# A gated FNet and GEGLU layer in split fp32: sum tiles in two places of their own, weight sums in place, loads and splits at fixed points of a pair

## The chip, the cores and the metric

The kernel runs on one core of a Trainium2 chip. The metric is device time in microseconds, the median over separate runs. One further run is recorded by the hardware profiler; all rows shown here come from that one execution. TensorE (PE) multiplies, VectorE (DVE) and ScalarE (ACT) prepare operands and take results, GpSimd (POOL) issues the stores and SyncE (SP) issues the loads.

## The reference

```python
g = sigmoid((x * gate_w).sum(-1, keepdims=True))     # x: 2048 x 640
a = Re(DFT_seq(DFT_hidden(x)))                       # dense real and imaginary DFT matrices
b = (gelu(x @ w_gate) * (x @ w_up)) @ w_down         # 640 -> 1728 -> 640, tanh gelu
return g * a + (1 - g) * b
```

Everything is fp32. The matrices of both DFTs are inputs.

## The kernel before, in words

**Arithmetic.** An fp32 product is made of three matmuls on fp32r operands: each operand is split into a high part (`high`, a copy on ScalarE, L75) and a low part (`low`, a subtraction on VectorE, L78), and `mm3` (L84 to L88) multiplies high by high, high by low and low by high into one PSUM bank of 128 x 512. Around that stand Strassen and Winograd forms: two blocks of 128 hidden units and two halves of a sequence half are combined so that fewer block products are needed, and sums of weights and of inputs are multiplied instead of the blocks themselves. Names with S, s or T, t are such sums.

**Stages.** The first stage splits x and its sums and computes the left-over blocks. Then come the gate and up products in pairs of hidden blocks. `gate_up` makes f = 1 and 2 one by one; `pair_first` and `chain` make pair p = 1; `whole_pair` (L508) makes each of the pairs p = 2, 3, 4, 5, which hold the blocks f = 2p+1 and 2p+2. After the pairs come the down products (the k stage), the DFT over the sequence (the c stage) and the DFT over the hidden dimension (the u stage).

**A whole pair.** `whole_pair` is a generator: it writes the pair's matmuls, seeds, copies and sums in a fixed order and yields numbers u = 3, 7, 10 ... 68. Between the yields the loop at L1151 to L1205 writes the other work of the pair: loads (`load_raw` for the weight tiles wa and wb of the next pair, `load_cross` for the input sums xx), `chain_parts` (the weight sums ws and their split, and wd), `fifth_parts` (the sums fs over the ws of both blocks, and their split fh), `pair_parts` (vs, vh, vl, ve, vq) and `plain_parts` (wp) for the next pair, and `extras`: the sums of a down weight chunk (`sum_wd`: loaded as dr and da, stored as wsd) and the logits of the gate (`load_z`: xz). Within the pairs the order on TensorE is as written (`in_order(PE)`); the order on the other engines is made by the scheduler of the framework, from the order in which the work is written and from what each instruction waits for.

A bank is copied with `seed` (L441): ScalarE copies a PSUM bank into another bank, and both go on as sums of their own. The seed px10 (L568) stands between the product s3 by t3 and the product a22 by t4: the latter accumulates on the copy.

**Places.** SBUF is handed out in slots of 4 KB per partition (`slot`, tag s4, 48 of them), 12 tiles of 2 KB (`mtile`) and 6 small ones (`wsmall`). A slot's next tile waits until the last reader of its former one is through, a store too. The s5 tile of a block (L539) holds the sum from which both its gated results are made; its four stores to DRAM (hT, by `keep`, L331) come at the pair's end, from L690 to L705. A down weight's sums are made into a further slot (`sums_left`, L707) and stored from there.

Of the kernel before, what the change touches and what calls it, by code (L numbers as in the profile page):

```python
# [30 lines left out]
def kernel(  # L31
# [33 lines left out]
    def slot(dt, shape, name):  # L65
        return pool.tile(shape, dt, tag="s4", name=name, bufs=48)

# [74 lines left out]
    def load_x(tp):  # L142


        n = f"{tp}"
        B, r = {}, {}
        src = xt[2 * tp : 2 * tp + 2]

        def tiles(t):
            for k in (1, 2):  # L150
                r[k, t] = pair(F32, f"xr{n}{k}{t}")
                B[k, t] = hl(f"x{n}{k}{t}")
            if t == 1:
                r[5], B[5] = pair(F32, f"xr{n}5"), hl(f"x{n}5")

        def load(t):
            for k in (1, 2):
                nc.sync.dma_start(r[k, t], src[t - 1, 2 * k - 2 : 2 * k].rearrange("d p c -> p d c"))
            nc.sync.dma_start(r[5][:, t - 1], src[t - 1, 4])

        def piece(d, t):

            raw = r[1 + d // 2, t][:, d % 2] if d < 4 else r[5][:, t - 1]
            return raw, src[t - 1, d], xpart(B, d, t)

        def tsum(i):
# [3 lines left out]
            tt(r[f"T{i}"], r[a], r[b], op=ALU.subtract)  # L170
# [12 lines left out]
        return B, tiles, load, piece, tsum, his, lows  # L183
# [52 lines left out]
    def chain_parts(f, raw, W):  # L236

        ra, rb = raw
        sm, *c = wchunk(f"ws{f}")
        g01, g23, u23 = ra[:, 0:2], ra[:, 2:4], ra[:, 5:7]  # L240
# [7 lines left out]

        def parts():
            split(*c, sm)  # L250
            split(d[:, 0], d[:, 1], rb[:, 1])
# [15 lines left out]
    def pair_parts(p, r0, r1):  # L267

        a, b = (r[:, 0:4].rearrange("q (j k) c -> q k j c", j=2) for r in (r0, r1))
        sm = slot(F32, [P, 4, 2, P], f"vs{p}")  # L270
        h, l = slot(F32R, [P, 4, 2, P], f"vh{p}"), slot(F32R, [P, 4, 2, P], f"vl{p}")
        e, q = slot(F32R, [P, 2, 4, P], f"ve{p}"), pool.tile([P, 2, 2, P], F32R, tag="m", name=f"vq{p}", bufs=12)
        tt(sm[:, 0], b[:, 0], b[:, 1], op=ALU.add)
        tt(sm[:, 2], a[:, 0], b[:, 0], op=ALU.subtract)
        tt(sm[:, 1], sm[:, 0], a[:, 0], op=ALU.subtract)
# [10 lines left out]
    def fifth_parts(p, W0, W1):  # L286
# [37 lines left out]

    tcross = {}

    def load_cross(J, i):
# [180 lines left out]
    def whole_pair(p, WP, Ws, raws):  # L508
# [98 lines left out]
        Z[0, 1] = seed(za, f"pz01{p}")  # L607
        yield 29
        fifth(Z[0, 0], 0, "u5", 1, 0)
        nc.scalar.activation(s5[0][:, 0], Z[0, 0], AF.Copy)  # L610
        plus(s5[0][:, 0], X[0, 0])
        prod(X[1, 0], 1, "S2", "T2", 0)
        state(1, 0)
# [11 lines left out]
        nc.scalar.activation(s5[0][:, 1], Z[0, 1], AF.Copy)  # L625
        plus(s5[0][:, 1], X[0, 1])
        m(Z[1, 0], 3, "a22", "t4")
# [128 lines left out]
    def gate_tile(row, tp, name):  # L756

        g = pair(F32, name)
        nc.sync.dma_start(g.rearrange("p t c -> p (t c)"), row[:, 2 * tp * T : 2 * (tp + 1) * T].to_broadcast([P, 2 * T]))
        return g  # L760

    def load_z(sb):

        r = slot(F32, [P, D], f"xz{sb}")
        nc.sync.dma_start(r, xz[sb])
        return lambda: nc.vector.tensor_tensor_reduce(r, r, gwb, 1.0, 0.0, ALU.mult, ALU.add, z[:, sb : sb + 1])

# [3 lines left out]
    def load_xn(sp):  # L771
# [9 lines left out]
        nc.sync.dma_start(r2, xn[sp, :, 3:5])  # L781
        sm = slot(F32, [P, 4, 256], f"xs{sp}")
        a11, a12, a22, a21 = r1[:, 0], r1[:, 1], r2[:, 0], r2[:, 1]
# [24 lines left out]
    def split_c(i):  # L808
# [3 lines left out]
        if b:  # L812
            s1 = pair(F32, f"csa{i}")
            tt(s1[:, 0], r1[:, 1], r1[:, 0], op=ALU.subtract)  # L814
            tt(s1[:, 1], r2[:, 0], r1[:, 1], op=ALU.subtract)  # L815
            s2 = pair(F32, f"csb{i}")
            tt(s2[:, 0], r2[:, 0], s1[:, 0], op=ALU.subtract)
# [16 lines left out]
    def load_k(i):  # L834
# [13 lines left out]
        elif b:  # L848
            nc.sync.dma_start(r[:, 0:2], wd[k, :, 6:8])
            nc.sync.dma_start(r[:, 2:8], wsd[k][:, 0:6])  # L850
            src = hT[tp][k]
        else:
            nc.sync.dma_start(r[:, 0:6], wd[k, :, 0:6])
            nc.sync.dma_start(r[:, 6:8], wsd[k][:, 6:8])
            src = hA[tp][k]
# [6 lines left out]
    def split_k(i):  # L862
# [18 lines left out]
        else:  # L881
            h, l = slot(F32R, [P, 8, P], f"kh{n}"), slot(F32R, [P, 8, P], f"kl{n}")
            split(h, l, r)
            names = ("A22", "S1", "S2", "S3") if b else ("A11", "A12", "e5", "S4")
            W = {name: (at((h, l), 2 * q), at((h, l), 2 * q + 1)) for q, name in enumerate(names)}
# [194 lines left out]
    sq = [lambda k=k: sum_wd(k) for k in range(NK)]  # L1080

    def extras(sums, logits):
        todo = [sq.pop(0)() for _ in range(sums) if sq]
# [6 lines left out]
    for f in (1, 2):  # L1090
        s5 = pair(F32, f"s5{f}")
        work = [gate_up(f, W, Bs[tp], tp, s5[:, tp]) for tp in range(2)]
# [28 lines left out]
    for i in range(2):  # L1121
        s5 = pair(F32, f"s5{f + i}")
        work = [chain(f + i, Ws[i], Bs[tp], tp, s5[:, tp], X[i, tp], s1[i, tp]) for tp in range(2)]
        for step in range(4):
# [13 lines left out]
            if (i, step) == (0, 2):  # L1138
                nraws = load_raw(f + 2), load_raw(f + 3)
            if (i, step) == (1, 0):  # L1140
                raws = nraws
                WP = pair_parts(2, raws[0][0], raws[1][0])
            if (i, step) == (1, 1):
                Ws = [plain_parts(f + 2 + i, raws[i][0]) for i in range(2)]
                for J in (2, 1):
                    load_cross(J, 1)
            if (i, step) == (1, 2):
                load_cross(2, 2)
            if (i, step) == (1, 3):
                load_cross(1, 2)  # L1150
    for p in range(2, NK):  # L1151
        f = 2 * p + 1
        more = p < NK - 1
        for J in (2, 1):
            load_cross(J, 4)
        with in_order(PE):
            for u in whole_pair(p, WP, Ws, raws):
                if u == 3:
                    parts = [chain_parts(f + i, raws[i], Ws[i]) for i in range(2)]
                if u == 7:  # L1160
                    parts[0]()
                    parts.append(fifth_parts(p, *Ws))
                    load_cross(3, 1)
                if u == 10:
                    WP[3] = parts[2]()
                    load_cross(3, 2)
                if u == 16:
                    parts[1]()
                    load_cross(3, 4)
                if u == 19:  # L1170
                    todo = extras(1, 2)
                if u == 23 and more:
                    nraws = load_raw(f + 2), load_raw(f + 3)
                if u == 29:
                    for do in todo[:1]:
                        do()
                    todo = todo[1:] + extras(p > 2, 2)
                if u == 38:
                    for do in todo:
                        do()  # L1180
                if more:
                    if u == 47:
                        nWP = pair_parts(p + 1, nraws[0][0], nraws[1][0])
                    if u == 56:
                        nWs = [plain_parts(f + 2, nraws[0][0])]
                        for J in (2, 1):
                            load_cross(J, 1)
                    if u == 62:
                        nWs.append(plain_parts(f + 3, nraws[1][0]))
                        load_cross(2, 2)  # L1190
                    if u == 65:
                        load_cross(1, 2)
                else:
# [377 lines left out]
```

## Time and profile before

| | |
|---|---|
| Median of three runs | 1031.0 us (1028.17, 1031.0, 1031.08) |
| The profiled execution | 1027.66 us |
| Its span | 1025.8 us |
| Mean granted clock of TensorE | 0.998 |
| TensorE busy | 1016.0 us, 99% of the span |
| VectorE busy | 807.0 us, 79% |
| ScalarE busy | 489.3 us, 48% |
| GpSimd busy | 140.7 us, 14% |
| DMA traffic | 265 MB, mean 258 GB/s |

The span is what the profiler saw between the first and last instruction; the execution's own time is 1.9 us longer. Busy shares hide where a stage waits. The 20-us windows of the trace show 89 or 90 matmuls in each full window but four: the first one (73), 200 to 220 us (78), 240 to 260 us (72), and 1000 to 1020 us (110, where the last ones are narrower).

In the rows of the timeline, the columns are start in us, duration in us, engine, source line, operation, written tile, read tiles, and shapes; a bracket gives the idle time before the instruction and what ended it. In the waits, the columns after the colon are total us, times and the longest wait. In the windows they are the stretch, its length, and busy us and instruction count of PE, PEld (weight loads), DVE, ACT and POOL, then the granted clock, the DMA share and GB/s. In the list of DMA issues the last number is the median time from issue to landing. In grouped rows of one tile they are the minimum, median and maximum duration in ns.

### The profile page before, as it was taken

How to read it: one execution, taken by the hardware profiler on the slowest of the kernel's cores; microseconds unless marked ns; L12 is line 12 of the kernel's file. 1: busy time of each engine (PE TensorE's matmuls, PEld its weight loads, DVE VectorE, ACT ScalarE, POOL GpSimd, SP SyncE). 2: the span in 40 equal slices, each digit the busy share in tenths (PEclk: the TensorE clock that was granted, in tenths of full speed). 3: DMA queues.
4: the chain of work that ended last, by engine and by line, in shares of the span. 5: the costliest groups of instructions: out<-in, count | busy, mean ns of one | idle time of the engine just before them, and what ended most of it. 6: DMA issues, size and time to landing. Idle time of an engine off the chain costs nothing.

```text
span 1025.8 us, 13092 instructions
## 1 busy us (share of the span) xinstructions
PE 1016.0 (99%) x4488; PEld 838.5 (82%) x4488; DVE 807.0 (79%) x1134; ACT 489.3 (48%) x654; POOL 140.7 (14%) x251
## 2 busy tenths in 40 slices
PE   9999999999999999999999999999999999999998
PEld 7888888787888888888888888888888888888887
DVE  6998797778785958976898976796598769697784
ACT  5445365454455547566355343443444345365430
POOL 0123131212121200100010011102100200021013
PEclk9999999999999999999999999999999999999999
DMA  8368697878698988867856679667966777897748
GB/s 300 120 211 290 248 326 269 298 258 308 235 336 310 301 285 278 282 257 254 322 190 237 212 244 331 228 216 259 324 231 215 269 270 286 292 323 217 276 92 134
DMA packets 87666, 265.00 MB, mean 258 GB/s; under 512 B 11088, under 2 KB 19312, under 8 KB 87600
## 3 DMA queue, kind: packets, MB, share of 16 engines
q1 hardware_dynamic: 65392, 194.47, 55.6%
q0 software_dynamic: 22064, 69.50, 19.8%
q8 instruction: 35, 0.57, 0.2%
q14 instruction: 31, 0.25, 0.1%
q10 hardware_dynamic: 144, 0.20, 0.1%
HBM read 194.38 MB, written 69.75 MB: 257 GB/s over the span
## 4 chain that ended last, share of the span: by engine, by line
PE 81%; issue 13%; POOL 4%; DMA 1%; DVE 1%; ACT 0%; POOLq 0%; DVEq 0%; ACTq 0%
PE pX L86 3%; PE pX L87 3%; PE pX L88 3%; PE pL L87 3%; PE pL L88 3%; PE pL L86 3%; PE pZ L88 2%; PE pZ L87 2%; PE pZ L86 2%; PE pV L87 2%; PE pV L88 2%; PE pV L86 2%; POOL hA L332 2%; POOL hT L332 1%; PE pR L87 1%
## 5 line engine op out<-in xcount | busy, mean ns | idle before, releaser
L75 ACT ACTIVATE ch<-csa 128x1024 fp32r<-128x1024 f32 x32 | 34.0, 1063 | 85.7 <-DVE csa L815 69.2
L75 ACT ACTIVATE ch<-cra 128x1024 fp32r<-128x1024 f32 x32 | 33.9, 1058 | 47.7 <-DVE cl L78 22.4
L78 DVE TENSOR_TENSOR cl<-crb,ch 128x1024 fp32r<-128x1024 f32 x32 | 39.1, 1221 | 16.3 <-ACT ch L75 14.7
L78 DVE TENSOR_TENSOR cl<-cra,ch 128x1024 fp32r<-128x1024 f32 x32 | 39.1, 1223 | 15.5 <-ACT ch L75 10.2
L88 PE MATMUL pL<-ch,xal 128*128 128x512 f32 x128 | 49.8, 389 | 0.0
L87 PE MATMUL pL<-cl,xah 128*128 128x512 f32 x128 | 49.8, 389 | 0.0
L86 PE MATMUL pL<-ch,xah 128*128 128x512 f32 x128 | 49.3, 389 | 0.0
L75 ACT ACTIVATE ch<-crb 128x1024 fp32r<-128x1024 f32 x32 | 33.8, 1057 | 25.0 <-PE pL L87 8.6
L78 DVE TENSOR_TENSOR cl<-csb,ch 128x1024 fp32r<-128x1024 f32 x32 | 39.2, 1224 | 3.1 <-ACT ch L75 1.2
L332 POOL DMA_DIRECT2D hA<-s x48 | 26.1, 544 | 104.7 <-DVE s L685 71.8
L78 DVE TENSOR_TENSOR cl<-csa,ch 128x1024 fp32r<-128x1024 f32 x32 | 39.0, 1220 | 1.2 <-ACT ch L75 0.8
L75 ACT ACTIVATE ch<-csb 128x1024 fp32r<-128x1024 f32 x32 | 34.0, 1063 | 9.3 <-DVE csb L818 5.8
L78 DVE TENSOR_TENSOR kl<-kw,kh 128x1024 fp32r<-128x1024 f32 (+1 forms) x26 | 31.4, 1209 | 5.8 <-ACT kh L75 5.8
L684 ACT ACTIVATE s<-s 128x512 f32<-128x512 f32 x20 | 12.7, 633 | 48.5 <-DVE s L530 33.0
L75 ACT ACTIVATE kh<-kw 128x1024 fp32r<-128x1024 f32 (+1 forms) x26 | 27.1, 1042 | 11.1 <-DVE kw L873 7.1
L928 POOL DMA_DIRECT2D out<-ks x12 | 6.5, 540 | 166.7 <-DVE ks L927 166.1
L332 POOL DMA_DIRECT2D hT<-s x48 | 26.0, 541 | 20.1 <-DVE s L703 5.5
L814 DVE TENSOR_TENSOR csa<-cra 128x512 f32<-128x512 f32 x32 | 21.9, 685 | 8.2 <-DMA wsu<-u2s 4.7
L86 PEld LDWEIGHTS pL<-ch,xah 128*128 128x128 f32 x128 | 24.0, 188 | 5.0
L87 PEld LDWEIGHTS pL<-cl,xah 128*128 128x128 f32 x128 | 24.0, 188 | 5.0
L88 PEld LDWEIGHTS pL<-ch,xal 128*128 128x128 f32 x128 | 24.0, 188 | 5.0
L1273 POOL DMA_DIRECT2D uA<-c x8 | 4.3, 541 | 170.2 <-DVE c L1360 170.0
(3120 smaller groups left out, 3442.1 us busy)
## 6 DMA issues: line engine op xcount, KB each, us to landing
cra<-in_ct SPq DMA_DIRECT2D x64, 512.0 KB, 4.4
crb<-in_ct SPq DMA_DIRECT2D x64, 512.0 KB, 5.3
xx<-xtd SPq DMA_DIRECT2D x42, 512.0 KB, 5.2
hA<-s POOLq DMA_DIRECT2D x48, 256.0 KB, 4.8
hT<-s POOLq DMA_DIRECT2D x48, 256.0 KB, 5.8
kr<-hA SPq DMA_DIRECT2D x24, 512.0 KB, 7.4
kr<-hT SPq DMA_DIRECT2D x24, 512.0 KB, 6.2
ux<-uA SPq DMA_DIRECT2D x24, 512.0 KB, 5.0
```

What stands on the lines that cost most here:

```text
L75: nc.scalar.activation(hi, raw, AF.Copy)
L78: nc.vector.tensor_tensor(lo, raw, hi.bitcast(F32), op=ALU.subtract)
L86: nc.tensor.matmul(ps, lh, rh, start=first, stop=False, skip_group_check=True)
L87: nc.tensor.matmul(ps, lh, rl, start=False, stop=False, skip_group_check=True)
L88: nc.tensor.matmul(ps, ll, rh, start=False, stop=last, skip_group_check=True)
L332: nc.gpsimd.dma_start(to[:, i], src)
L684: nc.scalar.activation(s2, s2, AF.Gelu_apprx_tanh)
L814: tt(s1[:, 0], r1[:, 1], r1[:, 0], op=ALU.subtract)
L928: nc.gpsimd.dma_start(out[2 * tp + t, e], src)
L1273: nc.gpsimd.dma_start(to[:, i], src)
```

## The change

**Sum tiles.** A new allocator `sumtile` has two places of 4 KB under a tag of its own, used in turn. It now holds the s5 tiles, the tile xr5 of the first stage, the raw down weights dr1 to dr4, the sums of x in `load_xn`, the sums csa and csb of the c stage and the gate rows gw. The slots go from 48 to 46. In `whole_pair` the s5 tiles are made where they are first written (at u = 29 and u = 38), no longer at the pair's start.

**Down weight sums in place.** `sum_wd` no longer takes a second tile: the four sums overwrite the loaded blocks, and the tile is stored to wsd. For this the four pairs of blocks lie in another order in `wd`, and `load_k` and `split_k` read and name them in that order.

**Fixed points.** `mark` remembers an instruction of an engine and `behind` orders later instructions after it on the same engine, without a semaphore. So the high split of fh stands behind the seed px10 on ScalarE; the dr sums, the logits and the first sums of `pair_parts` stand behind the sum of s5 and X on VectorE; the dr load stands behind the cross loads of (3, 1) and (3, 2) on SP. The points of the pair move: both of these cross loads at u = 10 (were 7 and 10); wp of the pair's second block at u = 10 of the pair itself (was u = 62 of the pair before); fh at u = 16 (was 10); extras done at u = 32 and 50 (were 29 and 38); the next raw weights at u = 32 (was 23); the cross loads of the next pair at 56, 62 and 65, always both (the last two were at the next pair's start).

```diff
 def slot(dt, shape, name):
-    return pool.tile(shape, dt, tag="s4", name=name, bufs=48)
+    return pool.tile(shape, dt, tag="s4", name=name, bufs=46)
+def sumtile(name):
+    return pool.tile([P, 2, T], F32, tag="s5", name=name, bufs=2)
...
+def mark(key):
+    passed[key] = nc.cur_bb.bb.instructions[-1].name
+def behind(key, n=1):
+    dep = mybir.DependencyInfo(mybir.DependencyClass.NoSync, mybir.DependencyReason.DATA)
+    for ins in nc.cur_bb.bb.instructions[-n:]:
+        tc.add_manual_dep(ins, passed[key], dep, reason="behind")
...
     # fifth_parts
-    split(h[:, 0], h[:, 1], e)
+    high(h[:, 0], e)
+    behind("act")
+    low(h[:, 0], h[:, 1], e)
...
     # whole_pair
-    s5 = [pair(F32, f"s5{f + i}") for i in range(2)]
+    s5 = [None, None]
...
     X[1, 0] = seed(xa_, f"px10{p}")
+    mark("act")
...
+    s5[0] = sumtile(f"s5{f}")
     fifth(Z[0, 0], 0, "u5", 1, 0)
     nc.scalar.activation(s5[0][:, 0], Z[0, 0], AF.Copy)
     plus(s5[0][:, 0], X[0, 0])
+    mark("dve")
...
     if i:
+        s5[1] = sumtile(f"s5{f + 1}")
...
 def sum_wd(k):
-    r, a21 = slot(F32, [P, 8, P], f"dr{k}"), wsmall(F32, f"da{k}")
+    r = slot(F32, [P, 8, P], f"dr{k}") if k in (0, NK - 1) else sumtile(f"dr{k}").rearrange("q t (k c) -> q (t k) c", c=P)
+    a21 = wsmall(F32, f"da{k}")
     nc.sync.dma_start(r, wd[k, :, :8])
+    if "sp" in passed:
+        behind("sp")
     nc.sync.dma_start(a21, wd[k, :, 8:])
-    return lambda: sums_left(f"d{k}", r, a21, wsd[k])
+    a12, a11, s2, a22 = (r[:, 2 * q : 2 * q + 2] for q in range(4))
+    def sums():
+        tt(a22, a21, a22, op=ALU.add)
+        if "dve" in passed:
+            behind("dve")
+        tt(s2, a22, a11, op=ALU.subtract)
+        tt(a11, a11, a21, op=ALU.subtract)
+        tt(a12, a12, s2, op=ALU.subtract)
+        nc.gpsimd.dma_start(wsd[k], r)
+    return sums
...
     # the pairs p = 2 to 5
-    for J in (2, 1):
-        load_cross(J, 4)
...
     if u == 7:
         parts[0]()
         parts.append(fifth_parts(p, *Ws))
-        load_cross(3, 1)
     if u == 10:
+        load_cross(3, 1)
+        load_cross(3, 2)
+        mark("sp")
+        Ws[1].update(plain_parts(f + 1, raws[1][0]))
+    if u == 16:
         WP[3] = parts[2]()
-        load_cross(3, 2)
-    if u == 16:
         parts[1]()
         load_cross(3, 4)
     if u == 19:
         todo = extras(1, 2)
-    if u == 23 and more:
-        nraws = load_raw(f + 2), load_raw(f + 3)
-    if u == 29:
-        for do in todo[:1]:
-            do()
-        todo = todo[1:] + extras(p > 2, 2)
-    if u == 38:
+    if u == 32:
+        for do in todo:
+            do()
+        if more:
+            nraws = next_raws(p + 1)
+    if u == 36:
+        todo = extras(not more, 2)
+    if u == 50:
         for do in todo:
             do()
     if more:
         if u == 47:
-            nWP = pair_parts(p + 1, nraws[0][0], nraws[1][0])
+            nWP = next_pair(p + 1, nraws)
         if u == 56:
-            nWs = [plain_parts(f + 2, nraws[0][0])]
-            for J in (2, 1):
-                load_cross(J, 1)
+            nWs = [next_plain(p + 1, nraws)]
+            next_cross(1)
         if u == 62:
-            nWs.append(plain_parts(f + 3, nraws[1][0]))
-            load_cross(2, 2)
+            next_cross(2)
         if u == 65:
-            load_cross(1, 2)
+            next_cross(4)
...
     # the host's layout of the down weights
-    "wd": np.concatenate([d[:, 0, :, 0:4:2], d[:, 1, :, 0:4:2], d[:, 0, :, 4:], ...], 2),
+    "wd": np.concatenate([d[:, 1, :, 0:4:2], d[:, 0, :, 0:4:2], d[:, 0, :, 4:], ...], 2),
```

The source lines in the rows below are those of each kernel; the changed kernel's are 3 to 60 higher for the same code. The number behind a tile's name and underscore only tells tiles apart.

The first place is VectorE near the start of pair p = 4 (blocks 9 and 10), where the weight sums ws10r are completed, ws9l is split and the sums fs begin. DMASW stands for a store that GpSimd issued. Before:

```order
L244 TENSOR_TENSOR ws10r_2255<-wa10_1963,ws10r_2255 128x256 [waits DVE_49]
L78 TENSOR_TENSOR ws9l_2248<-ws9r_2246,ws9h_2247 128x1024 [waits DMASW6_49,DMASW2_49,Activation_49]
L78 TENSOR_TENSOR wd9_2254<-wb9_1960,wd9_2254 128x128
L290 TENSOR_TENSOR fs4_2290<-ws10r_2255 128x128 [waits DMASW4_49]
L291 TENSOR_TENSOR fs4_2290<-ws9r_2246,ws10r_2255 128x128
```

and in the changed kernel:

```order
L247 TENSOR_TENSOR ws10r_2235<-wa10_2007,ws10r_2235 128x256 [waits DVE_49]
L81 TENSOR_TENSOR ws9l_2265<-ws9r_2228,ws9h_2264 128x1024 [waits Activation_49]
L81 TENSOR_TENSOR wd9_2234<-wb9_2004,wd9_2234 128x128
L296 TENSOR_TENSOR fs4_2270<-ws10r_2235 128x128 [waits DMASW2_49]
L297 TENSOR_TENSOR fs4_2270<-ws9r_2228,ws10r_2235 128x128
```

The order is the same; ws9l waits for its high part on ScalarE and no longer for two stores.

The second place is ScalarE in the same pair, from the split ws9h to the split ws10h: pv and px are seeds, s1 the copies on which the gelu works, fh4 the split of the sums fs4. Before:

```order
L443 ACTIVATE pv014_2270<-pva4_2226 128x512
L134 ACTIVATE s1004_2284<-px004_2238 128x512
L443 ACTIVATE px014_2278<-pxa4_2227 128x512
L75 ACTIVATE wd10_2263<-wb10_1964 128x128
L443 ACTIVATE pv104_2307<-pva4_2226 128x512
L75 ACTIVATE fh4_2309<-fs4_2290 128x512
L533 ACTIVATE s1004_2284<-s1004_2284 128x512
L134 ACTIVATE s1014_2319<-px014_2278 128x512
L443 ACTIVATE px104_2324<-pxa4_2227 128x512
L75 ACTIVATE ws10h_2256<-ws10r_2255 128x1024
```

and in the changed kernel:

```order
L461 ACTIVATE pv014_2248<-pva4_2208 128x512
L137 ACTIVATE s1004_2262<-px004_2220 128x512
L78 ACTIVATE wd10_2241<-wb10_2008 128x128
L461 ACTIVATE px014_2256<-pxa4_2209 128x512
L78 ACTIVATE wp10_2291<-wa10_2007 128x512
L461 ACTIVATE pv104_2285<-pva4_2208 128x512
L551 ACTIVATE s1004_2262<-s1004_2262 128x512
L461 ACTIVATE px104_2304<-pxa4_2209 128x512
L137 ACTIVATE s1014_2299<-px014_2256 128x512
L78 ACTIVATE fh4_2327<-fs4_2270 128x512
L137 ACTIVATE s1114_2307<-pxa4_2209 128x512
L78 ACTIVATE ws10h_2330<-ws10r_2235 128x1024
```

The split of wp10 has come in ahead of the seed pv10, and the seed px10 now stands ahead of the copy s101 and of fh.

The third place is ScalarE at the end of the first stage, where the sums xT11 to xT14 of x are split and block f = 1 begins; s51 is its sum tile. Before:

```order
L75 ACTIVATE xT11h_468<-xs11_466 128x1024
L75 ACTIVATE xT13h_473<-xs13_471 128x1024
L75 ACTIVATE xT12h_502<-xs12_500 128x1024
L75 ACTIVATE xT14h_508<-xs14_506 128x1024
L356 ACTIVATE ge12_530<-pg12_513 128x512
L134 ACTIVATE s11_0_580<-pX1_0_571 128x512
L134 ACTIVATE s11_1_591<-pX1_1_582 128x512
```

and in the changed kernel:

```order
L78 ACTIVATE xT11h_468<-xs11_466 128x1024
L420 ACTIVATE s51_570<-pZ1_0_572 128x512
L78 ACTIVATE xT13h_473<-xs13_471 128x1024
L78 ACTIVATE xT12h_502<-xs12_500 128x1024
L420 ACTIVATE s51_570<-pZ1_1_583 128x512
L78 ACTIVATE xT14h_508<-xs14_506 128x1024
L374 ACTIVATE ge12_530<-pg12_513 128x512
L137 ACTIVATE s11_0_580<-pX1_0_571 128x512
L137 ACTIVATE s11_1_591<-pX1_1_582 128x512
```

The two copies into s51 have moved ahead, one between the splits of xT11 and xT13, one ahead of xT14's. On TensorE nine matmuls of the S4 product of block 1 have moved ahead of the S2 product in the same place.

More of the change, by code (lines that the diff above doesn't have):

```diff
@@ L153, in tiles @@
             if t == 1:
-                r[5], B[5] = pair(F32, f"xr{n}5"), hl(f"x{n}5")
+                r[5], B[5] = sumtile(f"xr{n}5"), hl(f"x{n}5")
         def load(t):
@@ L238, in chain_parts @@
         ra, rb = raw
-        sm, *c = wchunk(f"ws{f}")
+        sm = slot(F32, [P, 8, P], f"ws{f}r")
         g01, g23, u23 = ra[:, 0:2], ra[:, 2:4], ra[:, 5:7]
@@ L249, in parts @@
         def parts():
+            c = [slot(F32R, [P, 8, P], f"ws{f}{n}") for n in "hl"]
             split(*c, sm)
@@ L626, in whole_pair @@
         plus(s5[0][:, 1], X[0, 1])
+        mark("dve")
         m(Z[1, 0], 3, "a22", "t4")
@@ L756, in gate_tile @@
     def gate_tile(row, tp, name):
-        g = pair(F32, name)
+        g = sumtile(name) if row is grd else pair(F32, name)
         nc.sync.dma_start(g.rearrange("p t c -> p (t c)"), row[:, 2 * tp * T : 2 * (tp + 1) * T].to_broadcast([P, 2 * T]))
@@ L765, in load_z, with logits @@
         nc.sync.dma_start(r, xz[sb])
-        return lambda: nc.vector.tensor_tensor_reduce(r, r, gwb, 1.0, 0.0, ALU.mult, ALU.add, z[:, sb : sb + 1])
+        def logits():
+            nc.vector.tensor_tensor_reduce(r, r, gwb, 1.0, 0.0, ALU.mult, ALU.add, z[:, sb : sb + 1])
+            if "dve" in passed:
+                behind("dve", 2)
+        return logits
     xa, xb = {}, {}
@@ L781, in load_xn @@
         nc.sync.dma_start(r2, xn[sp, :, 3:5])
-        sm = slot(F32, [P, 4, 256], f"xs{sp}")
+        sm = sumtile(f"xs{sp}").rearrange("q t (k c) -> q (t k) c", k=2)
         a11, a12, a22, a21 = r1[:, 0], r1[:, 1], r2[:, 0], r2[:, 1]
@@ L849, in load_k @@
             nc.sync.dma_start(r[:, 0:2], wd[k, :, 6:8])
-            nc.sync.dma_start(r[:, 2:8], wsd[k][:, 0:6])
+            nc.sync.dma_start(r[:, 2:8], wsd[k][:, 2:8])
             src = hT[tp][k]
@@ L853, in load_k @@
             nc.sync.dma_start(r[:, 0:6], wd[k, :, 0:6])
-            nc.sync.dma_start(r[:, 6:8], wsd[k][:, 6:8])
+            nc.sync.dma_start(r[:, 6:8], wsd[k][:, 0:2])
             src = hA[tp][k]
@@ L1080, with next_raws, next_pair, next_plain @@
     sq = [lambda k=k: sum_wd(k) for k in range(NK)]
+    def next_raws(p):
+        return [load_raw(2 * p + 1 + i) for i in range(2)]
+    def next_pair(p, raws):
+        return pair_parts(p, raws[0][0], raws[1][0])
+    def next_plain(p, raws):
+        return plain_parts(2 * p + 1, raws[0][0])
+    def next_cross(i):
+        for J in (2, 1):
+            load_cross(J, i)
     def extras(sums, logits):
@@ L1090 @@
     for f in (1, 2):
-        s5 = pair(F32, f"s5{f}")
+        s5 = sumtile(f"s5{f}")
         work = [gate_up(f, W, Bs[tp], tp, s5[:, tp]) for tp in range(2)]
@@ L1121 @@
     for i in range(2):
-        s5 = pair(F32, f"s5{f + i}")
+        s5 = sumtile(f"s5{f + i}")
         work = [chain(f + i, Ws[i], Bs[tp], tp, s5[:, tp], X[i, tp], s1[i, tp]) for tp in range(2)]
```

34 lines of the change are left out of this document (18 added, 16 removed).

## The prediction

> **What bounds the kernel now.** I read the page first: TensorE is busy for nearly all of the span, so a change pays only where it shortens time in which TensorE waits or runs at a lower clock. Work taken from another engine pays nothing by itself.
>
> ```profile
> PE 1016.0 (99%) x4488; PEld 838.5 (82%) x4488; DVE 807.0 (79%) x1134; ACT 489.3 (48%) x654; POOL 140.7 (14%) x251
> ```
>
> Second, the timeline of TensorE gives the first matmul of each whole pair p = 2, 3, 4, 5 and the first of the down stage. All four pairs run the same 207 matmuls.
>
> ```profile
> 142.91 0.39 PE L86 MATMUL pva<-x021h,ve 128*128 128x512 f32 x1
> ...
> 190.15 0.39 PE L86 MATMUL pva<-x021h,ve 128*128 128x512 f32 x1
> ...
> 239.91 0.39 PE L86 MATMUL pva<-x021h,ve 128*128 128x512 f32 x1
> ...
> 291.01 0.39 PE L86 MATMUL pva<-x021h,ve 128*128 128x512 f32 x1
> ...
> 338.08 0.39 PE L86 MATMUL kX<-kb0000h,kh 128*128 128x512 f32 x1
> ```
>
> The differences are 47.24, 49.76, 51.10 and 47.07 us. Pairs 2 and 5 agree (mean 47.16, or 0.227 us a matmul); pair 3 loses 2.60 and pair 4 loses 3.94, together 6.5 us. Third, the waits say what took it, and the windows what the clock did:
>
> ```profile
> PE px L86 <- ACT px L443: 4.6, 2, 2.3
> ...
> DVE ws7l L78 <- DMA hT<-s: 2.8, 1, 2.8
> ...
> DVE ws9l L78 <- DMA hT<-s: 2.8, 1, 2.8
> ```
> ```profile
> 200.00:205.00 5.00, 2.73 (x13) 1.93 (x12) 4.70 (x12) 3.71 (x7) 0.00 (x0) 1.00 0.81 271
> ...
> 254.00:256.00 2.00, 2.00 (x6) 1.51 (x5) 2.00 (x4) 1.66 (x4) 0.00 (x0) 0.54 1.01 375
> ```
>
> TensorE waits twice, 2.3 us each, once in pair 3 and once in pair 4. Behind the first wait the clock stays at 1.00; behind the second it falls to 0.54. So pair 4 lost about 2.6 to the wait and 1.3 to the clock. The timeline of pair 4 shows the chain, with the landing time of the stores from the list of DMA issues:
>
> ```profile
> 240.13 1.75 POOL L332 DMA_DIRECT2D hT<-s  x3
> ...
> 244.96 0.42 DVE L244 TENSOR_TENSOR ws10r<-wa,ws10r 128x256 f32<-128x256 f32 x1
> ...
> 248.19 1.23 DVE L78 TENSOR_TENSOR ws9l<-ws9r,ws9h 128x1024 fp32r<-128x1024 f32 x1 [2.81 <-DMA hT<-s]
> ...
> 250.56 0.39 PE L88 MATMUL pv<-x05h,wp 128*128 128x512 f32 x1
> ...
> 250.74 0.29 DVE L293 TENSOR_TENSOR fs<-ws9r,fs 128x128 f32<-128x128 f32 x1
> ...
> 251.06 0.63 ACT L75 ACTIVATE fh<-fs 128x512 fp32r<-128x512 f32 x1 [2.83 <-DVE fs L293]
> ...
> 252.59 0.59 ACT L443 ACTIVATE px<-pxa 128x512 f32<-128x512 f32 x1
> ...
> 253.24 0.50 PE L86 MATMUL px<-xx,vq 128*128 128x512 f32 x1 [2.29 <-ACT px L443]
> ```
> ```profile
> hT<-s POOLq DMA_DIRECT2D x48, 256.0 KB, 5.8
> ```
>
> VectorE is free at 245.38, but ws9l has been given the 4 KB slot of the previous pair's s5 tile, and that tile's store, issued from 240.13 on, takes 5.8 us to land. VectorE therefore begins ws9l at 248.19. The sums fs are late behind it, ScalarE waits for them with fh, and the seed px10 (L568, by way of L443), on which the next matmul rests, stands behind fh in ScalarE's order: 253.24 instead of about 250.8. Pair 5 shows the same piece without the blocked slot:
>
> ```profile
> 296.35 1.22 DVE L78 TENSOR_TENSOR ws11l<-ws11r,ws11h 128x1024 fp32r<-128x1024 f32 x1
> ...
> 298.90 0.28 DVE L293 TENSOR_TENSOR fs<-ws11r,fs 128x128 f32<-128x128 f32 x1
> ...
> 299.62 0.39 PE L88 MATMUL pxa<-x111h,vl 128*128 128x512 f32 x1
> ...
> 300.76 0.60 ACT L443 ACTIVATE px<-pxa 128x512 f32<-128x512 f32 x1
> ...
> 301.66 0.39 PE L88 MATMUL pv<-x05h,wp 128*128 128x512 f32 x1
> 301.89 0.39 PE L86 MATMUL px<-xx,vq 128*128 128x512 f32 x1
> ```
>
> The seed ends at 301.36 and TensorE wants it at 301.89: half a microsecond to spare, even unblocked.
>
> **The change part by part.** No matmul, sum, split or transfer is added or removed; all of it is order and place.
>
> First, the s5 tiles leave the 48 slots. In the new order ws7l, ws8l, ws9l and ws10l wait for ScalarE alone, no longer for a store. In pairs 3 and 4 VectorE then goes on as in pair 5. Gain between 0 and 2.60 in pair 3 and between 0 and 3.94 in pair 4; I take the upper ends, since the cause is removed and not shortened.
>
> Second, fh is put behind the px10 seed on ScalarE. The seed can then start when its bank is complete, about 300.05 in pair 5's times (299.62 and a matmul's 0.39), instead of 300.76. It ends about 300.7, and its cover grows from 0.5 to 1.2 us. fh itself is first multiplied some 75 matmuls into the pair, 17 us after its start, and is split about 11 us after it.
>
> Third, the second matrix's wp split is moved into the pair, ahead of the seed:
>
> ```profile
> L75 ACT ACTIVATE wp<-wa x10: 614/623/635, 88.4 to 281.1; 128x512 fp32r<-128x512 f32 x10
> L78 DVE TENSOR_TENSOR wp<-wa,wp x10: 682/684/693, 91.0 to 282.6; 128x512 fp32r<-128x512 f32 x10
> ```
>
> 0.62 on ScalarE falls into the hole ahead of the seed pv10, where it has nothing to do until the bank is done. 0.68 on VectorE stands right behind the last fs, so it ends at about 298.90 + 0.28 + 0.68 = 299.9; TensorE first needs it at 301.66. I cost it at nothing. Without those 1.8 us of cover it would cost at most its 0.68 in each of four pairs, 2.7.
>
> Fourth, the loads. SP now issues both xx3 tiles first, then the dr load, da, two wb, the third xx3, two xz and two wa; its dr load waits until the store of the first s5 has landed, and those behind it wait too. Landing times:
>
> ```profile
> xx<-xtd SPq DMA_DIRECT2D x42, 512.0 KB, 5.2
> ...
> wa<-in_wf SPq DMA_DIRECT2D x10, 512.0 KB, 6.6
> ...
> wsd<-d2s POOLq DMA_DIRECT2D x1, 512.0 KB, 6.9
> ```
>
> That store is issued about 1 us into the pair and lands near 7; dr lands near 13, and its sums come at 22. Counted in matmuls between the release of a slot and the first use, the cross tiles keep 12.9 us or more in pairs 2 to 5 (9.8 in the old order) and 7.1 in pair 1, against 5.2. No cost. The second wa is the one load that becomes later, and makes a rival.
>
> Fifth, the dr sums are made in place and their tile becomes the second s5 of the pair, which so waits for the wsd store. In pair 5's times:
>
> ```profile
> 312.92 0.69 DVE L530 TENSOR_TENSOR s<-s,px 128x512 f32<-128x512 f32 x1 [4.08 <-ACT s L610]
> ...
> 316.37 0.60 ACT L134 ACTIVATE s<-pxa 128x512 f32<-128x512 f32 x1 [0.72 <-PE pxa L88]
> ...
> 317.78 0.60 ACT L625 ACTIVATE s<-pz 128x512 f32<-128x512 f32 x1 [0.82 <-DVE pz L530]
> ...
> 319.57 0.39 PE L86 MATMUL pz<-x122h,ws11h 128*128 128x512 f32 x1
> ...
> 326.72 0.60 ACT L633 ACTIVATE s<-pz 128x512 f32<-128x512 f32 x1 [2.50 <-PE pz L88]
> ```
>
> The sums follow the row at 312.92 and end near 317; with the longest wsd landing of 6.9 the place is free at 324, and ScalarE writes it at 326.72. ScalarE's next instructions, the states and gelus of the pair's end, would queue behind it. No cost, with 2.7 us of cover.
>
> The down, sequence and last stages keep their order on TensorE, have two slots fewer, but their largest sums no longer use slots. I count nothing.
>
> Sum: the profiled execution took 1027.66 us, so 1027.66 - 6.5 = **1021.2** for its like. The median of the three runs is 1031.0, 3.3 above it. If that excess also lies in the two stalls (the halved clock behind one more wait would be 1.3 of it), it goes too, and the median comes to 1021.2; if it lies elsewhere, 1024.5. I take the middle, **1022.8 us**.
>
> **Rivals.** (1) The wait moves to the second wa tile; slower. Its slot is now released by the pair's 78th matmul, 17.8 us after the start, 6 us later than before, and its first user, the vq split, stands on ScalarE ahead of the copy of 317.78, for which the S4 product of 319.57 waits.
>
> ```profile
> L75 ACT ACTIVATE vq<-wa x5: 401/410/436, 82.2 to 269.9; 128x256 fp32r<-128x256 f32 x5
> ```
>
> The copy may start at about 318.8 and vq at 318.4, 27.4 after the start: the load may take 9.6 us. The rows say 6.6. With 12.5 it costs 2.9 and a clock fall of 1.3 in each of pairs 2, 3 and 4, 12.6 in all: 1035. It decides from landings above 9.6 and outweighs the gain above some 11.
>
> (2) The first stage loses part. On ScalarE the two s51 copies now stand ahead of xT14h and the s1 copies, and TensorE is already a little late there:
>
> ```profile
> 54.79 1.06 ACT L75 ACTIVATE xT14h<-xs 128x1024 fp32r<-128x1024 f32 x1 [1.21 <-DVE xs L170]
> ...
> 56.88 0.50 PE L86 MATMUL pX<-xT02h,ws1h 128*128 128x512 f32 x1
> ```
>
> In its favour, two copies of 0.60 and one split of 1.06 come ahead of what TensorE wants. Against it, nine matmuls of the S4 product (2.0 us) are also moved ahead of that use. Price 0 to 2.3, or 3.6 with a clock fall: up to 1026.4.
>
> (3) The halved clock has another cause than the wait, and stays: 5.2 is gained, 1024.1. For it: the same wait in pair 3 left the clock at 1.00. Against it: the fall begins within 2 us of the wait. The Trainium skill (TensorE: Matmul & The Clock Gate, Part 1) has the clock halved after an idle window of about 3.4 us, and the window runs freely; by its letter no gap here is long enough, and by that rule the 1.3 us would stay. Pair 4 speaks against the letter and for the free-running window.
>
> (4) The change does not do what it says: the seed stays late, because fh was not the last obstacle or VectorE is late for another reason, such as the moved wp split. Then 0 to 2.7 is left of the gain, 1028.3 to 1031.
>
> **How the numbers follow.** Forecast 0.70, (1) with the wsd wait 0.07, (2) 0.09, (3) 0.06, (4) 0.08. No change means within 0.3%, 3.1 us, of 1031.0, about what a measurement of this kernel can tell: 1027.9 to 1034.1. Forecast, (2) and (3) are faster, 0.85; I leave 0.03 of them for a slower set of runs: faster 0.82, same 0.11, slower 0.07. The range begins at 1020.2 (1021.2, and as much as 1 us of small waits in the first stage that the new order might also close) and reaches over the forecast's 1024.5 and most of (2) and (3) to 1027.5, which leaves out (4) and (1).
>
> **What would show it.** Right: pairs 3 and 4 take 47.1 to 47.3 us between first matmuls, the wait of px on ACT is gone from the list, ws7l and ws9l start as soon as VectorE has finished the sums, no clock under 0.99 behind 40 us, and px10's seed stands ahead of fh. Wrong: any wait of TensorE for pz or for s51 in the pairs ((1)), pX waiting for a copy at 55 to 65 us ((2)), a clock of 0.5 without a wait ((3)), or pairs of 49 us and more ((4)).

## The result and the profile after

The changed kernel takes 1021.5 us (median of four runs, 1021.01 to 1023.6) against 1030.99 (1028.17 to 1031.08): the ratio is 0.9918 with a 95% interval of 0.9896 to 0.9941, so it is faster by 9.5 us. A second set of five runs gave 1021.48. Two runs of the later sets, one of the kernel before (2089.42 us) and one of the last kernel in the table below (2102.74 us), fell in a slow state and are left out of the medians given here. The profiled execution took 1021.96 us, its span 1020.2, its mean granted clock 1.00. Forecast were 1022.8 us, between 1020.2 and 1027.5.

The windows of the changed kernel, cut at the first matmul of the pairs 2, 3, 4, 5 and of the down stage; the columns are as before, the last but two the granted clock:

```profile
144.43:191.55 47.12, 47.12 (x208) 38.77 (x207) 38.18 (x76) 23.93 (x43) 9.08 (x17) 1.00 0.84 281
191.55:238.47 46.92, 46.92 (x208) 38.85 (x207) 37.44 (x75) 24.07 (x42) 9.22 (x18) 1.00 0.79 271
238.47:285.39 46.92, 46.92 (x208) 38.85 (x207) 37.44 (x75) 24.07 (x42) 9.22 (x18) 1.00 0.78 268
285.39:332.47 47.08, 47.08 (x210) 38.87 (x208) 36.82 (x71) 29.97 (x48) 10.80 (x21) 1.00 1.00 362
```

TensorE is busy in every moment of the four pairs. They take 188.04 us where they took 195.17; pairs 3 and 4 fell from 49.76 and 51.10 to 46.92, which is 207 matmuls at 0.2267. What TensorE still waits for in the whole span:

```profile
PE pwarm L1078 <- DVE warm L1035: 1.2, 1, 1.2
PE px L89 <- DMA xx<-xtd: 0.5, 1, 0.5
PE pm L387 <- ACT x011h L78: 0.4, 1, 0.4
PE pm L387 <- ACT w0h L78: 0.2, 1, 0.2
```

The timeline of pair 4 shows the chain that was late before:

```profile
243.70 1.22 DVE L81 TENSOR_TENSOR ws9l<-ws9r,ws9h 128x1024 fp32r<-128x1024 f32 x1
...
246.24 0.28 DVE L299 TENSOR_TENSOR fs<-ws9r,fs 128x128 f32<-128x128 f32 x1
246.44 0.68 DVE L81 TENSOR_TENSOR wp<-wa,wp 128x512 fp32r<-128x512 f32 x1
247.57 0.58 ACT L461 ACTIVATE px<-pxa 128x512 f32<-128x512 f32 x1 [0.24 <-PE pxa L91]
...
248.55 0.63 ACT L78 ACTIVATE fh<-fs 128x512 fp32r<-128x512 f32 x1
...
249.35 0.39 PE L89 MATMUL px<-xx,vq 128*128 128x512 f32 x1
```

ws9l has no wait before it. The seed px10 waits only for its bank, ends at 248.15, and TensorE comes to it at 249.35: a cover (time to spare) of 1.2 us.

In the profiled executions the gain is only 5.7 us, since the changed one began worse: pair 2 starts at 144.43, not at 142.91. Of these 1.5 us, 0.5 is the wait for a cross tile (xx) in pair 1; in the first 20 us there were 69 matmuls, not 73. A second profile of the changed kernel has its pair 2 start at 142.69, with neither. The wait for the cross tile recurs all the same: it stands at the same matmul, with 0.3 to 0.7 us, in six later variants of the changed kernel, and in neither profile of before.

### The profile page after: what moved, and what is told of

Same layout as the page of the kernel before. It is cut to its first block, busy times and chain, and to the rows that moved or that the text cites. A ratio compares the mean times of both kernels' runs of the same rounds, so it can differ in the third digit from the quotient of the medians.

```text
span 1020.2 us, 13091 instructions
## 1 busy us (share of the span) xinstructions
PE 1014.4 (99%) x4488; PEld 838.2 (82%) x4488; DVE 805.0 (79%) x1134; ACT 491.3 (48%) x654; POOL 141.0 (14%) x251
## 4 chain that ended last, share of the span: by engine, by line
PE 98%; DMA 1%; ACT 0%; DVE 0%; SPq 0%; issue 0%
PE pX L89 4%; PE pX L91 4%; PE pX L90 4%; PE pL L91 3%; PE pL L90 3%; PE pL L89 3%; PE px L89 3%; PE px L90 3%; PE px L91 3%; PE pZ L91 2%; PE pZ L90 2%; PE pZ L89 2%; PE pV L91 2%; PE pV L90 2%; PE pV L89 2%; PE pY L91 1%
## 5 line engine op out<-in xcount | busy, mean ns | idle before, releaser
L548 DVE TENSOR_TENSOR s<-s,px 128x512 f32<-128x512 f32 x12 | 8.2, 686 | 27.9 <-ACT s L630 25.9
```

Of the source, the lines that this page charges most:

```text
L548: tt(a, a, c, op=ALU.add)
```

## The experiments

Pair times are the differences between first matmuls, in us, of one profiled execution each; the medians come from several runs each, but for the row that says one run (before: 1029.6 to 1031.0 in the different sets).

| Kernel | Median | p = 2 | p = 3 | p = 4 | p = 5 |
|---|---|---|---|---|---|
| before | 1030.99 | 47.24 | 49.76 | 51.10 | 47.07 |
| before, second profile | (1028.45, one run) | 48.86 | 50.08 | 49.31 | 47.07 |
| the change | 1021.5 | 47.12 | 46.92 | 46.92 | 47.08 |
| the change, second profile | 1021.48 | 47.11 | 46.92 | 46.92 | 47.07 |
| before + fh behind the seed | 1029.73 | 48.77 | 50.60 | 49.76 | 47.08 |
| before + places for the pairs' s5 | 1040.49 | 54.37 | 49.26 | 50.75 | 47.07 |
| before + all places, sums in place | 1041.05 | 55.74 | 52.69 | 53.17 | 47.08 |
| change without places | 1027.72 | 52.98 | 46.91 | 46.92 | 47.08 |
| change, places for s53, s54 alone | 1045.06 | 47.13 | 53.88 | 54.67 | 50.37 |
| change, fh early, wp behind it | 1027.75 | 48.98 | 48.24 | 48.23 | 48.39 |
| change, fh early, wp ahead of it | 1022.4 | 47.10 | 47.10 | 47.17 | 47.93 |

### fh behind the seed, alone

```diff
 # the kernel before, fifth_parts
-    split(h[:, 0], h[:, 1], e)
+    high(h[:, 0], e)
+    behind("act")          # marked at the seed px10
+    low(h[:, 0], h[:, 1], e)
 # WP[3] = parts[2]() at u == 16, not 10
```

> The kernel before with one edit: the high split of fh stands behind the seed px10 on ScalarE. Theory A: ws7l and ws9l still wait 2.8 us for the stores, and the gelu ahead of the seed still waits for a VectorE sum behind ws9l, so the seed comes about 1.1 us earlier than before; the wait of TensorE shrinks from 2.3 to about 1.2 in pairs 3 and 4, and the time falls by 2 to 4 us, 1027 to 1029. Theory B: both waits are gone, 1021 to 1024. Theory C: no change, 1031.

Measured: 1029.73 us, ratio 0.9992 (0.9979 to 1.0005): no change, where theory A had 1027 to 1029. The timeline of this kernel, pairs 3 and then 2:

```profile
200.73 1.23 DVE L78 TENSOR_TENSOR ws7l<-ws7r,ws7h 128x1024 fp32r<-128x1024 f32 x1 [3.54 <-DMA hT<-s]
...
203.93 0.58 ACT L456 ACTIVATE px<-pxa 128x512 f32<-128x512 f32 x1
...
204.57 0.50 PE L86 MATMUL px<-xx,vq 128*128 128x512 f32 x1 [1.77 <-ACT px L456]
```
```profile
156.06 0.63 ACT L75 ACTIVATE fh<-fs 128x512 fp32r<-128x512 f32 x1 [2.58 <-DMA hT<-s]
...
159.67 0.50 PE L86 MATMUL px<-xT03h,ws5h 128*128 128x512 f32 x1 [1.55 <-ACT s L134]
```

fh no longer stands in the way, and the wait falls from 2.3 to 1.8 in both pairs, not to 1.2; ws7l still waits for the stores. And in pair 2, which had no such wait, now fh itself has been dealt the slot of an s5 tile, and TensorE waits 1.55 for a copy behind it. The two shorter waits save about 1.0, and pair 2 loses 1.5. (Pair 3, at 50.60, also has a fall of the clock behind its wait; pair 4, at 49.76, has none.) Theory B, that the order alone was the obstacle, is out.

### The places, alone

```diff
 # the kernel before; e1: the s5 tiles of the whole pairs
-    ... name=name, bufs=48)
+    ... name=name, bufs=46)
-    s5 = [pair(F32, f"s5{f + i}") for i in range(2)]
+    s5 = [sumtile(f"s5{f + i}") for i in range(2)]
 # e8: all tiles that the change puts there, s5 made where it is written,
 #     sums of the down weights in place; order and load points as before
```

> The kernel before with one edit: the s5 tiles of the whole pairs lie in two places of their own (46 slots beside them); order, load points and weight sums as before. Theory A (the slot of ws7l and ws9l was the whole cause): pairs 3 and 4 take 47.1 to 47.3 us between first matmuls and the wait of px on the seed is gone, so the time is that of the full change, 1021 to 1024. Theory B (fh ahead of the seed px10 was the obstacle): pairs 3 and 4 keep 49 us or more, 1028 to 1031. Theory C (the moved load and split points do it): likewise unchanged. A fourth way: here ws5l of pair 2 waits for stores of pair 1's s5, so the wait may reappear in pair 2 (49.7) and leave 1024 to 1027.

> The places and the sums in place of the change, with the order, the load points and the fh of the kernel before. No ws, wp or fh of a whole pair waits for the store of an s5 tile here. Theory (the slot decides): the seed px10 is in time and pairs 3 and 4 lose nothing there; but the old points hang on slots too, of which there are two fewer, so other waits may stand in the pairs: 1021 to 1030, with no wait of px on the seed. Theory C: pairs 3 and 4 keep 49 us and more with that wait, 1028 to 1031.

Measured: 1040.49 us (1.0104, 1.0087 to 1.0121) and 1041.05 (1.0109, 1.0092 to 1.0126), slower than before and outside every expected range. In the first, from the timelines of pairs 2 and 3:

```profile
162.90 1.23 DVE L81 TENSOR_TENSOR ws5l<-ws5r,ws5h 128x1024 fp32r<-128x1024 f32 x1 [4.81 <-DMA hT<-s]
...
230.41 0.43 DVE L714 TENSOR_TENSOR d3s<-da,dr 128x256 f32<-128x256 f32 x1 [4.57 <-DMA wsd<-d2s]
...
233.40 0.50 PE L89 MATMUL pz<-x122h,ws7h 128*128 128x512 f32 x1 [2.02 <-ACT s L628]
```

s53 and s54 are still slots, and ws5l of pair 2 falls on one of them, as the fourth way expected. In pairs 3 and 4 the wait on the seed is gone, but a down weight sum now lies on the slot of the former one, waits for its store, and holds up the s5 copy behind it. That isn't all of this kernel's loss: its pair 2 starts at 148.29, 5.4 us later than before, with waits of TensorE for cross tiles in pair 1 (1.4, 0.8 and 1.4 us), and three more of them (2.4 in all) stand in pair 2. The edit also takes two slots from the pool while few tiles leave it; whether that is their cause was not tried. In the second kernel no early tile waits for an s5 store; from its waits between 140 and 310 us and SP's own:

```profile
DVE dr L746 <- DMA da<-in_wd: 8.2, 3, 4.2
...
ACT vh L78 <- DVE vs L282: 7.3, 3, 5.8
PE px L89 <- ACT s L137: 7.1, 2, 3.9
...
PE pz L89 <- ACT s L642: 5.3, 1, 5.3
...
DVE vs L278 <- PE pz L91: 4.7, 1, 4.7
```
```profile
SPq L739 <- DMA hT<-s: 22.7, 3, 9.2
```

The dr load, which now needs an s5's place, waits at the head of SP's queue for that s5's store, up to 9.2 us, and da stands behind it. In pairs 3 and 4 VectorE has the dr sum early in its order and waits for da 4.2 and 3.5 us; behind it stands the sum of pxa, and behind that, on ScalarE, the copies for which TensorE waits (the two waits of px). Pair 2, the dearest, is another case: VectorE waits 4.7 us for a matmul before it can write the first vs sum, ScalarE stands 5.8 us at vh behind these sums, and the copy of pz, for which TensorE waits 5.3, stands behind vh. The clock falls behind all three waits. So the places cure the seed, as theory A says, and without the moved points they bring a new wait of the same kind in two pairs and leave room for another in the third.

### The points, alone

```diff
 # the changed kernel
-    ... tag="s4", name=name, bufs=46)
+    ... tag="s4", name=name, bufs=48)
 def sumtile(name):
-    return pool.tile([P, 2, T], F32, tag="s5", name=name, bufs=2)
+    return slot(F32, [P, 2, T], name)
```

> The changed kernel with one part undone: the tiles of the two places are ordinary slots again (48 of them); sums in place, order and load points as in the change. The two stores are not among what ws5l to ws12l wait for here either, since the moved allocations deal the slots out differently. Theory A in its narrow form (two places of their own are needed) has the waits back, 1028 to 1031. In its wide form (what matters is only on whose slot ws7l and ws9l fall, and any shift of allocations may mend it) and by theory C the time is that of the full change, 1021 to 1024. Theory B: also 1021 to 1024.

The sums in place and the later s5 tiles stay in this kernel too. Measured: 1027.72 us, 0.9982 (0.9971 to 0.9994) of before. Neither expected range held. Pairs 3 to 5 are as in the full change, 46.9 to 47.1; pair 2 takes 52.98. Its timeline:

```profile
156.83 0.63 ACT L78 ACTIVATE wp<-wa 128x512 fp32r<-128x512 f32 x1 [5.59 <-DMA hT<-s]
...
158.00 0.80 PE L89 MATMUL pv<-xx,vq 128*128 128x512 f32 x1 [4.12 <-ACT pv L461]
```

Here it is wp6 of pair 2 that lies on the slot of s53, and the expectation had followed only what the ws tiles wait for. The seed pv10 stands behind it. So the moved points alone free ws7l and ws9l, since they change how the slots are dealt out, and one bad deal is left. To try the reading, only s53 and s54 were given places, which deals the bad slots to pairs 3 and 4:

```diff
 # the changed kernel
 def sumtile(name):
+    if name not in ("s53", "s54"):
+        return slot(F32, [P, 2, T], name)
     return pool.tile([P, 2, T], F32, tag="s5", name=name, bufs=2)
```

> The changed kernel with only s53 and s54, the sum tiles of pair 1, in the two places; all others are slots again (46). Dealt out like this, wp6 of pair 2 no longer waits for a store of an s5 tile, but wp8 of pair 3 waits for those of s56 and wp10 of pair 4 for those of s58, which are stored last. Theory (the slot decides): pair 2 at 47.1; in pairs 3 and 4 ScalarE stands at wp and the seed pv10 behind it is 2 to 4 us late, as in pair 2 of the version without places: 50 to 53 us each, in all 1027 to 1034. Theory C (the load and split points do it, the places only matter once): 1021 to 1024.

Measured: 1045.06 us, 1.0148 (1.0129 to 1.0166). From its waits between 140 and 356 us:

```profile
PE pv L91 <- ACT pv L463: 10.1, 2, 5.5
ACT wp L80 <- DMA hT<-s: 5.0, 2, 2.9
DVE ws8r L246 <- DMA hT<-s: 4.9, 1, 4.9
DVE ws10r L246 <- DMA hT<-s: 4.9, 1, 4.9
```

Pair 2 is whole at 47.13, and pairs 3 and 4 stand at the tiles that were named, and at ws8r and ws10r, which were not: 53.88 and 54.67. The place was right, and theory C, by which the time would have stayed at 1021 to 1024, is out; the price and the total were higher than expected. Pair 5, with ws11l on such a slot, loses 3.3 too. And pair 2 starts at 148.63, 4.2 us later than in the change, behind waits for cross tiles in pair 1 (1.4, 0.8 and 1.2 us) like those of the first kernel with places alone.

### The order of fh and wp

```diff
 # the changed kernel: fh split at u == 10, without behind("act")
 # e3: fh written ahead of wp      e6: wp written ahead of fh
```

> The changed kernel with one part undone: fh is split at u = 10 again and stands ahead of the seed px10 on ScalarE. Theory A: the seed ends about 0.5 us before TensorE wants it, as in pair 5 before, so nothing is lost: 1021 to 1023, pairs at 47.1. Theory B: the waits are back in pairs 3 and 4, 1028 to 1031. Theory C: 1021 to 1023.

> The changed kernel with fh ahead of the seed px10 again, but with wp still ahead of both, so that only fh changes sides. If putting fh behind the seed has no worth of its own, as forecast (0.5 us of cover without it): 1021 to 1024 and pairs at 47.1. If the seed is late with fh ahead of it: a wait of px on the seed of 0.3 to 1 us in each of four pairs, 1023 to 1028.

Measured: 1027.75 us (0.9979, 0.9969 to 0.999) and, over five runs, 1022.4 (0.9932, 0.9917 to 0.9948). The first misses all expectations: the scheduler had put wp behind the seed. Its waits on TensorE:

```profile
PE pv L89 <- ACT wp L78: 3.0, 4, 1.2
...
PE pv L91 <- DVE wp L81: 0.8, 4, 0.3
```

It tells nothing of fh, but prices wp: TensorE waits for it in all four pairs, which take 193.84 us together, 5.8 more than in the change. With wp ahead (the second kernel) the seed is in time with fh in front of it, with a cover of 0.4 us in pair 2 and 1.0 in the others. Its pair 5 has a wait of 0.4 for an s5 copy, its pair 1 one of 0.7 for a cross tile, and 1022.4 stands 0.9 over the change. Whether fh has a small worth of its own can't be told from that.

### What a late seed costs, and the clock

```diff
 # the changed kernel, whole_pair
     mark("late")                                   # behind the seed pv10
+    for _ in range(n):                             # n = 4, 9, 14
+        nc.scalar.activation(ident, ident, AF.Copy)
+        behind("late")
+        mark("late")
     X[1, 0] = seed(xa_, f"px10{p}")
+    behind("late")
```

> The changed kernel with the seed px10 made late: 4 copies of a 128x128 tile onto itself stand ahead of it on ScalarE in each of the four whole pairs. By the rows the seed then ends some 0.3 us after TensorE wants it. Theory A with a clock that only falls after longer waits: 4 times 0.3, about 1 us over the changed kernel, no window with a lower clock. Rival (the clock falls after any wait): up to 4 times 1.3 more.

> As the former, with 9 copies and, in the order that results, the gelu of s101 ahead of the seed too: a wait of about 2.5 us in each of four pairs, as long as that of pairs 3 and 4 before. Theory: 4 times 2.5 and the fall of the clock by chance, as the wait lies against a free-running window, in about two of four pairs, 1.3 to 1.6 each: 12.5 to 13.5 us over the changed kernel, 1034. Rival, that the clock does not hang on the wait: 10 us over, 1031.5, and no fall in any pair.

> As the former, with 14 copies: a wait of about 4 us in each of four pairs. Theory: a whole window of 3.4 us can be idle, so the clock falls in every pair or nearly so: 4 times (4 + 1.6) = 22 us over the changed kernel, 1044. Rival, that the clock does not hang on the wait: 16 us over, 1037.5.

Measured: 1022.69, 1037.06 and 1045.9 us, where about 1022.5, 1034 and 1044 were expected. With 4 copies TensorE does not wait for the seed, against the expectation (pairs 47.09, 47.16, 47.14, 47.31). With 9 it waits 1.92, 2.01, 2.16 and 2.01 us, a little less than meant; the pairs of that kernel:

```profile
145.63:194.79 49.16, 47.24 (x209) 38.78 (x208) 38.60 (x76) 26.42 (x52) 9.05 (x17) 1.00 0.80 274
194.79:245.62 50.83, 48.82 (x209) 39.91 (x207) 37.64 (x75) 26.43 (x51) 9.20 (x18) 0.97 0.73 251
245.62:296.58 50.96, 48.80 (x208) 39.92 (x207) 37.73 (x75) 26.53 (x51) 9.20 (x18) 0.97 0.75 250
296.58:347.58 51.00, 48.99 (x209) 39.92 (x208) 37.01 (x71) 32.33 (x57) 10.76 (x21) 0.97 0.93 334
```

The first pair loses 2.0 us, just the wait, and its clock stays at 1.00. The others lose 3.9 to 4.0: the clock falls behind the wait. Their waits are 0.1 to 0.2 longer than the first pair's, so a fall costs about 1.8. With 14 copies, pairs 2 and 3:

```profile
144.17:197.66 53.49, 49.50 (x208) 40.48 (x207) 38.56 (x76) 27.84 (x57) 9.05 (x17) 0.94 0.74 247
197.66:249.94 52.28, 48.56 (x209) 39.79 (x207) 37.65 (x75) 27.98 (x56) 9.21 (x18) 0.97 0.71 243
```

Four waits (15.3 us in all, 3.7 to 4.0 each) and four falls; pairs 3 and 5 lose 5.4, pairs 2 and 4 lose 6.4 to 6.5. In the pairs of both kernels the clock never fell without a wait before it. The rival that the clock does not hang on the wait is out.

### Both kernels once more

> The kernel before once more, for a second profile. If the 3.3 us by which its median stands above its profiled execution lie in the two stalls (a halved clock behind the first wait too), an execution of about 1031 shows pair 3 at 51 us as well and a clock near 0.5 behind it, with all other stages as in the first profile. If they lie elsewhere, pairs 3 and 4 stay at 49.8 and 51.1 and another stage is 3 us longer.

> The changed kernel once more, beside the next three. By the theory as it now stands (a tile that is needed early in a pair must not lie on the slot of an s5 tile whose store is still under way) nothing in it can wait for such a store: 1021 to 1024, pairs 2 to 5 at 46.9 to 47.2 us. If the 7 us of the first two profiles were luck with landing times, a pair of 48 us and more shows up here.

The kernel before, in an execution of 1028.45 us, is not one of about 1031. It has no fall of the clock in its pairs, not even behind its wait of 2.59 in pair 3, but it has a third wait, in pair 2:

```profile
172.25 1.06 ACT L75 ACTIVATE vh<-vs 128x1024 fp32r<-128x1024 f32 x1 [2.16 <-DVE vs L276]
173.21 0.58 ACT L625 ACTIVATE s<-pz 128x512 f32<-128x512 f32 x1
```
```profile
173.84 0.50 PE L86 MATMUL pz<-x122h,ws5h 128*128 128x512 f32 x1 [1.30 <-ACT s L625]
...
206.00 0.50 PE L86 MATMUL px<-xx,vq 128*128 128x512 f32 x1 [2.59 <-ACT px L443]
```

The copy of pz stands on ScalarE behind vh, which waits for the vs sums, late on VectorE. The change puts the first vs sums behind the sum of s5 and X, and in its pair 4 ScalarE makes the copy (265.25) ahead of vh (268.75). So the loss of before is not at fixed places: it wanders between three pairs and the clock. In these two executions it comes to 7.1 and 7.3 us over the changed kernel's pairs. The changed kernel's second profile repeats its pair times to 0.01 us. It has waits of pX for copies, 1.7 us in all, near 654 and 753 us, long after the pairs, that the first did not have; these remain.

## Why the prediction was right

**The chain and its size: right.** The wait on the slot's store, through ws9l, fs and fh to the seed, is gone, with a cover of 1.2 us as worked out. The pairs gained 7.1 us where 6.5 was forecast; pairs 2 to 4 came to 46.9 and 47.1, a little under the 47.16 that I took as undisturbed.

**The median's excess: mis-sized.** "I take the middle" between 1021.2 and 1024.5; the median is 1021.5. Nearly all of the 3.3 us by which the median stood above the profiled execution went too. The second profile of before shows one place where it can come from, the wait of 1.3 in pair 2, beside falls of the clock by chance (about 1.8 us each in the kernel with 9 copies; counted matmul by matmul, 1.6 in pair 4 of before; not the 1.3 that I got by subtracting pair 3, which has slow matmuls of its own). The granted clocks of the single runs tell more. In three later sets of before (47 runs), 25 runs have a clock of 0.998, as the profiled execution with its one fall has, and take 1029.0 us on the mean; 16 have 0.996 and take 1031.0. The changed kernel's runs all have 0.999 or 1.000. So about 2.0 of the 3.3 goes with the clock, as much as one more fall. The rest is open, and no profile caught an execution at the median. The middle of 1022.8 was a choice and not a reading; that it came within 1.3 us of the result is luck.

**What does it: the step that was incomplete.** Under "First" I put the gain to the places alone, and costed the other parts at nothing, as rearrangement. The runs show neither part has the gain alone: places without points 1040 to 1041, points without places 1027.7, fh without both 1029.7, all together 1021.5. "No cost" for the dr load that waits for an s5 store holds only because its sums are put behind the sum of s5 and X; in the old order pairs 3 and 4 lost 5.8 and 6.3 us behind the same wait, the clock's falls included. The sums in place were not undone by themselves, so their own part is not known. And the deal of slots, which frees ws7l and ws9l, changes with any moved allocation.

**The cross tiles of pair 1: a small cost, not none.** Under "Fourth" they had 7.1 us against a landing of 5.2. In the first profile of the change the load that TensorE waited for, issued at 100.3, took 9.4 us to land, and the wait is 0.5:

```profile
xx<-xtd SPq DMA_DIRECT2D x1, 512.0 KB, 9.4
```

**wp: the bound was too low.** Without cover I allowed its 0.68 on VectorE in each pair, 2.7. Measured without cover: 5.8. Both splits stand in a row there, and TensorE waits for each.

**fh: as forecast**, no measurable worth by itself once wp stands ahead; the 0.5 us of cover that was read without it came to 0.4 to 1.0.

**The rivals.** (1) The second wa was not late: its two loads landed in 4.9 us (median, pair 3) and 4.7 (pair 4), against the 9.6 allowed:

```profile
wa<-in_wf SPq DMA_DIRECT2D x2, 512.0 KB, 4.9
```

The place that it named was a real one all the same: the S4 product waited there for the s5 copy in both kernels with places alone and in the second profile of before, each time for other work ahead of the copy. (2) TensorE waits for no copy at 55 to 65 us in either profile. (3) is out by the runs with a late seed. The Trainium skill (TensorE: Matmul & The Clock Gate, Part 1) asks for about 3.4 us of idleness before the clock is halved; here waits of 2.01, 2.01 and 2.16 us were enough, while one of 1.92 and, in the second profile of before, one of 2.59 were not. The measurement decides on the length: 2 us can do. That it is a matter of chance at such lengths fits the window that the same section describes as running freely, but no run here shows such a window. (4) did not happen.

## What to carry to other kernels

A tile in a shared pool waits for the last reader of the tile before it, and a store that is issued late is such a reader; list which tiles needed early fall on slots of tiles stored late, for every kind of tile and not only for the one that stalls now. Places of their own remove the wait by construction, but whatever is loaded into them inherits it, so its consumers must be moved behind the point at which it can be there. Where margins are half a microsecond, judge an edit only together with the order it leads to: each part of this change alone left most of the gain out or made the kernel slower.

## What the runs showed of the hardware

A wait of TensorE of 2 us costs 2 or 4 us. In the two kernels with 9 and 14 copies the clock fell to one half behind three of four waits of 1.9 to 2.2 us and behind all four of 3.7 to 4.0. In the other traces it also fell behind a wait of 1.77 (pair 3 of the kernel with fh behind the seed) and stayed at full behind one of 2.59 (second profile of before). The windows behind the first wait (1.92) and the second (2.01) of the kernel with 9 copies show it:

```profile
160.00:162.00 2.00, 2.00 (x11) 1.62 (x10) 1.99 (x4) 1.85 (x4) 0.00 (x0) 1.00 0.98 370
209.00:211.00 2.00, 2.00 (x6) 1.51 (x6) 1.79 (x3) 1.24 (x3) 0.00 (x0) 0.50 0.36 94
```

The same work ran at 11 matmuls in 2 us and at 6.
